# A plan for operand building and Sinkhorn beside unit 0's end, larger token blocks in unit 0, and a reordered lead-in, in a one-core attention and mixture-of-experts kernel

## The chip, the cores and the metric

The kernel runs on one core of a Trainium2 chip. The metric is the device time of one execution in microseconds (us), median of the runs made. The engines are named as the profile names them: PE is TensorE (its weight loads are PEld), DVE is VectorE, ACT is ScalarE, POOL is GpSimd, and SP is the engine whose queue issues the transfers. Each engine works off its own list of instructions in order; semaphores tie the lists together.

## The reference

Three parts follow each other, all in float32. The attention has 2 batches, 8 heads, 768 tokens and head size 64, so 1536 tokens of width 512 come out of it.

```
k_sum = k.reshape(B, H, nb, 32, D).max(axis=3);  v_sum = v.reshape(B, H, nb, 32, D).mean(axis=3)
scores = concat([where(|i - j| < 16, q k^T / 8, -1e9), q k_sum^T / 8 + log(32)])
x = softmax(scores) @ concat([v, v_sum])                  # (1536, 512)
logits = x @ w_gate;  P = exp(logits - logits.max())      # (1536, 8)
for _ in range(8):                                        # Sinkhorn
    P /= P.sum(1) + 1e-9;  P /= P.sum(0) + 1e-9;  P *= N / E
y = sum over e of P[:, e] * (relu(x @ w1[e]) @ w2[e])      # 8 experts, 512 -> 1024 -> 512
h = y @ w_in                                              # 512 -> 2048
out = ((a0 + a1 h + a2 h^2 + a3 h^3) / (1 + |b0| |h| + |b1| h^2 + 1e-6)) @ w_out
```

## The kernel before

**Numbers in two halves.** Each large float32 operand is held as a high half (`h`) and a low half (`l`, the rest), and each product takes three matmuls (lines 166 to 168 and 948 to 950). `xh` and `xl` are the attention's output, `w1h`, `w1l`, `w2h`, `w2l` the weights, `hh`, `hl` the hidden layer. Making a low half needs its high half first, as a rule on ACT, and then a subtraction on DVE or POOL.

**Units.** The eight experts are cut into 16 units of 512 hidden columns, and the last part into four. Unit 0 runs beside the attention in blocks of tokens. Its jobs stand in the list `mains`: per block four `g1` (one for each 128 hidden columns; 12 matmuls, then ReLU on ACT and `hl` on DVE) and per 128 tokens one `g2` (12 matmuls of 512 columns, copied to `acc` by ACT). Units 1 to 15 run as 30 steps `v`, each over the two halves `j` of the tokens: `block(v, j)` forms its hidden layer by seven products (named by their sums X, Y and Z) of prepared sums instead of eight, and its second layer (`g2w`, tiles `p_v`) is spread over the next block, six jobs of six matmuls. I write block (0,0), (0,1), (1,0) for them.

**Operands of the seven products.** From `xh` and `xl` `t_queue(0..3)` builds `th` and `tl`, each for 192 tokens of both halves: four additions (`parts`, tiles `b`), four differences (`all_sums`), three casts on ACT with three differences (`outs`). `t1_queue(0..3)` rewrites part of `xh`, `xl` (tiles `c`): two additions, a difference, a cast, a difference. On the weights' side `w_sums` (tile `S`, four operations on POOL) and `w_op` (seven per step `v`, tiles `wA` and `wS`, high and low half) and `w2_op` (two per step, `w2h_v` and `w2l_v`, on POOL).

**What sets the order.** Everything is written out by hand: an instruction stands in its engine's list where the Python code comes to it. In the attention there is one round `s` per 64 query tokens: scores of `s`, values of `s-3`, transposition of `s-2`, normalization of `s-1`, exponentials of `s`, the key window of `s+1` (`kw`, POOL), then jobs from `todo` at that round and `main(s, 0.8)` twice, which takes jobs from `mains` as far as their costs fit the credit. `ready` holds a block of unit 0 back until its tokens are through. After the last round the rest of `mains` is taken one by one, with one entry of the list `beside` after each: weights' sums, logits, and the work of `t_queue(0, 1)` and `t1_queue(0, 1)`. The other two of each go in at `step(v)`, two at a time, in block (0,0) and on.

**Sinkhorn.** Ten jobs (`sk_max_b`, `sk_first`, eight `sk_step`) run at calls of `tick`, one call per `step`, six per block. Each `sk_step` sends one small matmul (`csp`) to PE that needs DVE's column sums (`cs`), and DVE then goes on with its result. In the kernel before all ten may run from the first call on.

**The lead-in.** Three groups of 256 keys and one of 256 queries are loaded (`load_nat`), copied to token order (`by_token`, two DVE copies), transposed on PE, placed (`place` for keys, `place_q` for queries) and reduced to block maxima (`block_keys`, DVE), group after group; then the first round starts.

Of the kernel before, what the change touches and what calls it, by code (L numbers as in the profile page):

```python
# [22 lines left out]
def kernel(  # L23
# [244 lines left out]
    with ExitStack() as actx:  # L268
# [83 lines left out]
        def by_token(nm, b, i):  # L352

            t = nat[nm, b, i]
            n = len(ordered)
            g = NTT - 2 * (4 - n if n < 4 else 1 + n % 2)
            ordered.append(n)
            for par in range(2):
                r, x = acc[g + par].rearrange("p (h d) -> p h d", h=H), t[:, :, par, :]
                if n >= 4:  # L360
                    pcopy(r, x)
                else:
                    nc.vector.tensor_copy(r, x)
            nat[nm, b, i] = acc[g:g + 2]
# [118 lines left out]
        load_nat(k, "k", 0, 1)  # L483
        load_nat(k, "k", 0, 2)
        make_identity(nc, ident)
        for j in range(2):
            for t_ in qz:
                nc.gpsimd.memset(t_[j * D:(j + 1) * D, :, :, 1 - j, :], 0.0)
        nc.vector.memset(ones, 1.0)
        nc.vector.memset(wavg, 0.0)  # L490
        for m in (wavg[:, NB - LT // BLK:NB],):
# [11 lines left out]
            nc.vector.memset(t_, 0.0)  # L503
        for t_ in vx:
            nc.vector.memset(t_, 0.0)
        for i, m in enumerate(masks):
            nc.gpsimd.memset(m, 0.0)
            nc.gpsimd.memset(m[:, :, SO:CO], math.log(BLK))
            if i == 0:
                nc.gpsimd.memset(m[:, :, 0:WIN], NEG)  # L510
            if i == 2:
                nc.gpsimd.memset(m[:, :, QT + WIN:WK], NEG)
            for j in range(2):
                mm = m[j * QT:(j + 1) * QT, 0, 0:WK]
                nc.gpsimd.affine_select(
                    out=mm, in_=mm, compare_op=ALU.is_ge, fill=NEG, base=-1,
                    pattern=[[1, WK]], channel_multiplier=-1,
                )
                nc.gpsimd.affine_select(
                    out=mm, in_=mm, compare_op=ALU.is_ge, fill=NEG, base=2 * WIN - 1,  # L520
                    pattern=[[-1, WK]], channel_multiplier=1,
                )

        new_q(0, 0)
        for i in range(NL):
            by_token("k", 0, i)
            load_nat(v, "v", 0, i)
            load_vx(i)
# [3 lines left out]
            if i == 0:  # L532
                by_token("q", 0, 0)
                for par in range(2):
                    place_q(qT[0, 0], par, transpose8("q", 0, 0, par, True))
                window(0, 1)
            block_keys(0, i)
        load_nat(q, "q", 0, 1)
        for g in range(2):
            dma_w(0, 1, g)  # L540
        window(0, 2)
        todo = {}
        SW = [3, 3, 4, 4, 4, 4, 5, 5]

        def at(s, f, *args):
            todo.setdefault(s, []).append(lambda: f(*args))


        for i in range(NL):
            at((i + 1) // 3, sum_v, 0, i)  # L550
# [47 lines left out]
        for s in range(NQ + AV):  # L598
            if s < NQ:
                scores(s)  # L600
            if s >= AV:
                av(s - AV)
                if s - AV + 3 < NQ:
                    load_vx(s - AV + 3)
            if 0 <= s - AV + 1 < NQ:
                trans(s - AV + 1)
            if 0 < s <= NQ:
                norm(s - 1)
            if s < NQ:
# [8 lines left out]
            main(s, 0.8)  # L618
        assert not todo


# [187 lines left out]
    tjobs = {0: [], 1: []}  # L809

    def t_part(nm, i, tag, k, t, eng=None):
        o = i // 2 * HT + t * NW + i % 2 * TPIECE
# [5 lines left out]
    def t_queue(i):  # L818
# [3 lines left out]

        def parts():
            b[11], b[12] = t_part("b11", i, "s1", 0, 0), t_part("b12", i, "s2", 0, 1)
            b[22], b[21] = t_part("b22", i, "s3", 1, 1, nc.vector), t_part("b21", i, "s1", 1, 0, nc.vector)

        def sums(r, x, y):
            nc.vector.tensor_sub(b[r], b[x], b[y])
# [11 lines left out]
            for a in ((1, 12), (0, 22), (2, 21)):  # L840
                out(*a)

        tjobs[i // 2] += [parts, all_sums, outs]

    def t1_queue(i):
        o = i // 2 * HT + NW + i % 2 * TPIECE
# [8 lines left out]
            nc.scalar.copy(h, b[11])  # L855
            nc.vector.tensor_sub(l, b[11], h.bitcast(F32))

        tjobs[i // 2] += [parts, out]

    wop = {}  # L860
    wS = {}
# [61 lines left out]

    def step(v):
        tick(v > 1)
        for f in tjobs[1][:2]:
            f()
        del tjobs[1][:2]

    def block(v, j):  # L930

# [93 lines left out]
                if extra:  # L1025
                    extra(b, c)

    for i in (0, 1):
        t_queue(i)
    for i in (0, 1):  # L1030
        t1_queue(i)
    for i in (2, 3):
        t_queue(i)
    for i in (2, 3):
        t1_queue(i)
    beside = [lambda: w_sums(0), lambda: logit_step(0), lambda: w_op(0, 0), lambda: logit_step(1), lambda: w_op(0, 1)]
    for f in tjobs.pop(0):
        beside.append(f)
    beside[6:6] = [lambda: logit_step(2)]
    beside[9:9] = [lambda: logit_step(3)]  # L1040
    while mains:
# [60 lines left out]
```

## Time and profile before

| what | value |
|---|---|
| median of 3 runs (lowest, highest) | 1456.67 us (1455.76, 1458.33) |
| the profiled execution | 1455.68 us, span of its trace 1454.0 us |
| granted PE clock, mean over the span | 0.981 of full speed |
| first score product (score tile 0) starts | 20.92 us |
| ninth score product (tile 8) starts: mark A | 64.06 us |
| first `g1` of unit 0 after the last attention product | 146.54 us |
| X of block (0,0) starts: mark B | 187.05 us |
| X of block (1,0) starts: mark C | 256.11 us |
| X of block (2,0) starts | 287.39 us |

Times within the trace count from the span's start. Busy time of PE is a sum of overlapping matmuls, so it is read together with the start of the next matmul. A clock of 1.00 is 2.4 GHz, 0.50 is 1.2 GHz.

### The profile page before, as it was taken

What the parts mean: (1) busy time and instruction counts of PE and PEld (TensorE: products, weight loads), DVE (VectorE), ACT (ScalarE), POOL (GpSimd) and SP (SyncE); (2) the same over time, 40 slices, a digit from 0 to 9 for tenths busy, and PEclk for the clock granted to TensorE, in tenths of its full rate; (3) what the DMA queues carried; (4) which work ended last, traced back from release to release, by engine and by line L of the source; (5) the groups of instructions that cost most, each with busy time, mean ns of one, the idle gap of its engine ahead of it and who ended that gap; (6) DMA issues with size and microseconds to landing.
All of it is one profiled execution on the core that took longest, in us unless ns stands there. A gap on an engine that the chain in (4) does not pass through costs nothing.

```text
span 1454.0 us, 19477 instructions
## 1 busy us (share of the span) xinstructions
PE 1382.1 (95%) x7195; PEld 1217.7 (84%) x7195; DVE 1074.5 (74%) x1858; ACT 505.2 (35%) x1106; POOL 839.6 (58%) x1042
## 2 busy tenths in 40 slices
PE   5899946999999999999999999999999999999998
PEld 3778835888898888888888889888888998888886
DVE  5676368567777777767776777777776579999996
ACT  4666321232122122222221222212212258776764
POOL 5641365357677767666776767766766333555541
PEclk9899967999999999999999999999999999999999
DMA  6731001112111222111222122212211110111002
GB/s 160 180 98 40 1 14 44 37 52 62 62 62 60 69 76 62 59 55 62 76 60 68 62 62 62 66 61 77 62 62 52 48 44 1 47 33 38 30 0 87
DMA packets 90094, 85.55 MB, mean 59 GB/s; under 512 B 22928, under 2 KB 70032, under 8 KB 90000
## 3 DMA queue, kind: packets, MB, share of 16 engines
q1 hardware_dynamic: 90000, 84.32, 19.5%
q8 instruction: 57, 0.93, 0.3%
q14 instruction: 37, 0.30, 0.1%
HBM read 72.76 MB, written 11.53 MB: 58 GB/s over the span
## 4 chain that ended last, share of the span: by engine, by line
PE 61%; DVE 20%; POOL 8%; ACT 6%; DMA 2%; issue 2%; SPq 0%; ACTq 0%; POOLq 0%; DVEq 0%
PE p_v L168 10%; PE p_v L167 9%; PE p_v L166 9%; PE X L948 5%; PE X L949 5%; PE X L950 5%; DVE r L206 4%; PE Y L949 2%; PE Y L950 2%; PE Y L948 2%; DVE ta L209 2%; DVE ab L203 2%; DVE ab L192 2%; PE p L166 2%; PE p L167 2%; PE p L168 2%
## 5 line engine op out<-in xcount | busy, mean ns | idle before, releaser
L1009 DVE SCALAR_TENSOR_TENSOR acc<-p_v,Pt,acc 128x512 f32<-128x512 f32 x336 | 250.1, 744 | 76.8 <-PE p_v L168 75.1
L168 PE MATMUL p_v<-w2h_v,hl_v 128*128 128x512 f32 x720 | 286.4, 398 | 0.0
L167 PE MATMUL p_v<-w2l_v,hh_v 128*128 128x512 f32 x720 | 285.0, 396 | 0.0
L166 PE MATMUL p_v<-w2h_v,hh_v 128*128 128x512 f32 x720 | 282.0, 392 | 0.0
L956 ACT ACTIVATE hh_v<-s 128x384 fp32r<-128x384 f32 x180 | 94.7, 526 | 355.7 <-DVE s L971 202.6
L957 DVE SCALAR_TENSOR_TENSOR hl_v<-s,hh_v 128x384 fp32r<-128x384 f32 x180 | 126.4, 702 | 104.9 <-ACT hh_v L956 104.9
L168 PEld LDWEIGHTS p_v<-w2h_v,hl_v 128*128 128x128 f32 x720 | 135.3, 188 | 28.9
L736 POOL TENSOR_SCALAR ce<-ce 128x256 uint32<-128x256 uint32 x64 | 69.1, 1079 | 152.8 <-DVE ce L730 152.8
L166 PEld LDWEIGHTS p_v<-w2h_v,hh_v 128*128 128x128 f32 x720 | 135.8, 189 | 17.0
L167 PEld LDWEIGHTS p_v<-w2l_v,hh_v 128*128 128x128 f32 x720 | 135.4, 188 | 16.9
L213 POOL TENSOR_TENSOR hl<-ta,hh 128x512 fp32r<-128x512 f32 (+1 forms) x52 | 63.1, 1214 | 141.2 <-ACT hh L212 139.2
L963 ACT COPY s<-X 128x384 f32<-128x384 f32 x60 | 28.8, 480 | 248.5 <-PE X L950 248.5
L111 POOL TENSOR_SCALAR wS<-S 128x256 fp32r<-128x256 f32 x116 | 57.9, 499 | 98.2 <-PE X L950 96.4
L166 PE MATMUL p<-xh,w1h 128*128 128x512 f32 (+3 forms) x304 | 107.2, 353 | 0.0
L168 PE MATMUL p<-xh,w1l 128*128 128x512 f32 (+3 forms) x304 | 106.0, 349 | 0.0
L167 PE MATMUL p<-xl,w1h 128*128 128x512 f32 (+3 forms) x304 | 106.0, 349 | 0.0
L112 POOL TENSOR_TENSOR wS<-S,wS 128x256 fp32r<-128x256 f32 x120 | 96.4, 804 | 16.3 <-ACT wS L109 6.6
L166 PE MATMUL p<-w2h,hh 128*128 128x512 f32 x240 | 95.3, 397 | 2.4 <-DVE acc L238 2.3
L168 PE MATMUL p<-w2h,hl 128*128 128x512 f32 x240 | 94.3, 393 | 0.1
L167 PE MATMUL p<-w2l,hh 128*128 128x512 f32 x240 | 94.3, 393 | 0.0
L948 PE MATMUL X<-th,wS 128*128 128x384 f32 x240 | 80.8, 337 | 4.9 <-ACT s L963 4.9
L112 POOL TENSOR_TENSOR w2l_v<-sb,w2h_v 128x512 fp32r<-128x512 f32 x60 | 81.0, 1350 | 5.0
(189 smaller groups left out, 3436.1 us busy)
## 6 DMA issues: line engine op xcount, KB each, us to landing
sa<-in_moe_w_dram SPq DMA_DIRECT2D x30, 512.0 KB, 3.5
sb<-in_moe_w_dram SPq DMA_DIRECT2D x30, 512.0 KB, 3.8
cv<-in_moe_w_in_dram SPq DMA_DIRECT2D x32, 256.0 KB, 3.7
cv<-in_moe_w_out_dram SPq DMA_DIRECT2D x32, 256.0 KB, 3.3
f_in<-cf SPq DMA_DIRECT2D x32, 128.0 KB, 2.3
f_out<-cf SPq DMA_DIRECT2D x32, 128.0 KB, 1.8
s<-f_in SPq DMA_DIRECT2D x8, 512.0 KB, 3.4
s<-f_out SPq DMA_DIRECT2D x8, 512.0 KB, 3.6
```

The lines of the kernel that those rows point to most:

```text
L112: nc.gpsimd.tensor_sub(lo, src, hi.bitcast(F32))
L166: nc.tensor.matmul(ps, lhsT=sh, rhs=mh, start=(i == 0), stop=False)
L167: nc.tensor.matmul(ps, lhsT=sh, rhs=ml, start=False, stop=False)
L168: nc.tensor.matmul(ps, lhsT=sl, rhs=mh, start=False, stop=(i == n_k - 1))
L213: nc.gpsimd.tensor_sub(hl[:, :n], ta, hh[:, :n].bitcast(F32))
L736: nc.gpsimd.tensor_scalar(out=e, in0=e, scalar1=896, scalar2=0, op0=ALU.subtract, op1=ALU.max)
L948: nc.tensor.matmul(ps, lhsT=w[:, 0, t], rhs=mh, start=start and t == 0, stop=False, **go)
L949: nc.tensor.matmul(ps, lhsT=w[:, 0, t], rhs=ml, start=False, stop=False, **go)
L950: nc.tensor.matmul(ps, lhsT=w[:, 1, t], rhs=mh, start=False, stop=t == 1, **go)
L956: nc.scalar.activation(hh, src, AF.Relu)
L957: nc.vector.scalar_tensor_tensor(out=hl, in0=src, scalar=0.0, in1=hh.bitcast(F32), op0=ALU.max, op1=ALU.subtract)
L1009: nc.vector.scalar_tensor_tensor(out=a, in0=ps, scalar=Pt[:, g, e:e + 1], in1=a, op0=ALU.mult, op1=ALU.add)
```

## The change

Five things are altered.

1. Lead-in: of the two copies of `by_token` one goes to ACT, of the two placings of a key group one goes to DVE; `place_q` moves behind the copy of the second key group; masks 1 and 2 and the zeroing of the second query buffer are made later (the mask of the last rows in round 4); the second query group is loaded into a staging tile and so ahead of the value groups' use; it is transposed in round 2 instead of 3.
2. Unit 0's weights are split in rounds 3 to 6, two parts each, before in rounds 3 to 5 (two, four, two).
3. Unit 0's token blocks are 256, 256, 256, 384, 384, before 128, 128, 256, 256, 384, 384. The credit per round goes from 1.6 to 1.4.
4. After the last round a table `plan` of eleven groups is laid over the remaining jobs of `mains` up to the last `g1`. It holds `t_queue(0..2)`, `parts` and `all_sums` of the fourth, and `t1_queue(0, 1)`. Two of the four additions of `parts` move from DVE to POOL. Five pieces (`rest`) are left for the first five `step`s.
5. Sinkhorn's ten jobs get due calls 4, 6, 8, 10, ... 22.

```diff
         def load_nat(src, nm, b, i):
-            if (nm, b, i) == ("q", 0, 0):
-                t = apool.tile([P, NP, LT], F32, tag="kT", name="q_0_0", bufs=4)
+            if nm == "q" and b == 0 and i < 2:
+                if i:
+                    t = spool.tile([P, KC, 2 * P], F32, tag="stg", name="q_0_1")
+                else:
+                    t = apool.tile([P, NP, LT], F32, tag="kT", name="q_0_0", bufs=4)
...
-                if n >= 4:
+                if n >= 5:
                     pcopy(r, x)
+                elif par:
+                    nc.scalar.copy(r, x)
                 else:
                     nc.vector.tensor_copy(r, x)
...
+        def place_k(i):
             new_k(0, i)
             for par in range(2):
-                place(kT[0, i], par, transpose8("k", 0, i, par, True), 1.0, True)
+                place(kT[0, i], par, transpose8("k", 0, i, par, True), 1.0)
...
-        SW = [3, 3, 4, 4, 4, 4, 5, 5]
+        SW = [3, 3, 4, 4, 5, 5, 6, 6]
...
+        at(4, make_mask, 2)
...
-        order = [(3, "q", 0, 1)] + [(8 + i, "k", 1, i) for i in range(NL)]
+        order = [(2, "q", 0, 1)] + [(8 + i, "k", 1, i) for i in range(NL)]
...
-        for n in (P, P, 2 * P, 2 * P, HB, HB):
+        for n in (2 * P, 2 * P, 2 * P, HB, HB):
...
-            main(s, 0.8)
+            main(s, 0.7)
...
-        if g2q and g2q[0][0] <= point[0] or len(jobs) > 9 or not g2q:
+        if g2q and g2q[0][0] <= point[0] or not g2q:
             run_job()
...
-    jobs += [(0, sk_max_b), (0, sk_first)]
-    jobs += [(0, lambda i=i: sk_step(i == 7)) for i in range(8)]
+    jobs += [(4, sk_max_b), (6, sk_first)]
+    jobs += [(8 + 2 * i, lambda i=i: sk_step(i == 7)) for i in range(8)]
...
-            b[22], b[21] = t_part("b22", i, "s3", 1, 1, nc.vector), t_part("b21", i, "s1", 1, 0, nc.vector)
+            b[22], b[21] = t_part("b22", i, "s3", 1, 1), t_part("b21", i, "s1", 1, 0)
...
     def step(v):
         tick(v > 1)
-        for f in tjobs[1][:2]:
+        for f in rest[:1]:
             f()
-        del tjobs[1][:2]
+        del rest[:1]
...
+    plan = [
+        [lambda: logit_step(0), T[0][0]],
...
+        [T[3][1]],
+    ]
+    g1s = len(mains) - HB // P
...
+    for m in range(len(mains)):
         mains.pop(0)[2]()
-        if beside:
-            beside.pop(0)()
-    for f in beside:
-        f()
-    for i in range(2, len(OPS)):
-        w_op(0, i)
+        while plan and m + 1 >= g1s * (12 - len(plan)) // 11:
+            for f in plan.pop(0):
+                f()
+        if m == g1s - 1:
+            assert not plan
+            for i in range(2, len(OPS)):
+                w_op(0, i)
     dma_sub(1, 1)
+    rest = [T[3][2], T[6][0], T[7][0], T[6][1], T[7][1]]
```

How the table moves instructions shows at two engines. First DVE at unit 0's end. `hl_768_0` is the low half of unit 0's hidden layer for the block that starts at token 768, `b_0` are the tiles of `t_queue(0)`, `tl` its results, `Pt` the logits. Before:

```order
L181 SCALAR_TENSOR_TENSOR hl_768_2_1838<-p_0_768_2_1824,hh_768_2_1837 128x384
L181 SCALAR_TENSOR_TENSOR hl_768_3_1858<-p_0_768_3_1844,hh_768_3_1857 128x384
L649 TENSOR_TENSOR Pt<-Pt,lgt_1861 128x32
L815 TENSOR_TENSOR b_0_1914<-xh,xl 128x384
L815 TENSOR_TENSOR b_0_1916<-xh,xl 128x384
L649 TENSOR_TENSOR Pt<-Pt,lgt_1932 128x32
L181 SCALAR_TENSOR_TENSOR hl_1152_0_1964<-p_0_1152_0_1950,hh_1152_0_1963 128x384
L828 TENSOR_TENSOR b_0_1910<-b_0_1912,b_0_1910 128x384
```

Of the change:

```order
L674 TENSOR_TENSOR Pt<-Pt,lgt_1716 128x32
L853 TENSOR_TENSOR b_0_1689<-b_0_1691,b_0_1689 128x384
L853 TENSOR_TENSOR b_0_1691<-b_0_1693,b_0_1691 128x384
L853 TENSOR_TENSOR b_0_1693<-b_0_1693,b_0_1689 128x384
L853 TENSOR_TENSOR b_0_1695<-b_0_1695,b_0_1693 128x384
L181 SCALAR_TENSOR_TENSOR hl_768_0_1774<-p_0_768_0_1760,hh_768_0_1773 128x384
L181 SCALAR_TENSOR_TENSOR hl_768_1_1791<-p_0_768_1_1777,hh_768_1_1790 128x384
L858 TENSOR_TENSOR tl_1652<-b_0_1691,th_1649 128x2x192
```

The differences of `t_queue(0)` stand eight jobs of unit 0 earlier, ahead of the block at token 768 instead of behind the first `g1` of the block at 1152, and the additions are gone from DVE's list.

Second POOL in block (0,0). `wA_1` and `wS_1` are weight operands of step 1, `b_2`, `b_3`, `c_2`, `c_3` tiles of `t_queue` and `t1_queue`, `w2h_v_0` the first second-layer weight, which the first `g2w` needs. Before:

```order
L815 TENSOR_TENSOR b_2_2150<-xh,xl 128x384
L815 TENSOR_TENSOR b_2_2152<-xh,xl 128x384
L111 TENSOR_SCALAR wA_1_2168<-sa_2126 128x256
L112 TENSOR_TENSOR wA_1_2168<-sa_2126,wA_1_2168 128x256
L815 TENSOR_TENSOR b_3_2188<-xh,xl 128x384
L815 TENSOR_TENSOR b_3_2190<-xh,xl 128x384
L111 TENSOR_SCALAR wS_1_2213<-S_2140 128x256
L112 TENSOR_TENSOR wS_1_2213<-S_2140,wS_1_2213 128x256
L815 TENSOR_TENSOR c_2_2260<-xh,xl 128x384
L815 TENSOR_TENSOR c_2_2262<-xh,xl 128x384
L111 TENSOR_SCALAR w2h_v_0_2273<-sb_1256 128x512
```

Of the change:

```order
L111 TENSOR_SCALAR wA_1_2120<-sa_2088 128x256
L112 TENSOR_TENSOR wA_1_2120<-sa_2088,wA_1_2120 128x256
L840 TENSOR_TENSOR c_2_2124<-xh,xl 128x384
L840 TENSOR_TENSOR c_2_2126<-xh,xl 128x384
L111 TENSOR_SCALAR wS_1_2145<-S_2102 128x256
L112 TENSOR_TENSOR wS_1_2145<-S_2102,wS_1_2145 128x256
L840 TENSOR_TENSOR c_3_2149<-xh,xl 128x384
L840 TENSOR_TENSOR c_3_2151<-xh,xl 128x384
L111 TENSOR_SCALAR w2h_v_0_2177<-sb_1120 128x512
```

Four additions of `t_queue(2)` and `t_queue(3)` no longer stand here; four of `t1_queue` still do, between the weights' operations.

## Rows read from the trace of the kernel before

**Rows 1.** The page's table of 40 slices of 36.35 us: PE's line.

```profile
PE   5899946999999999999999999999999999999998
```

**Rows 2.** Windows between marks: length; PE, PEld, DVE, ACT, POOL busy (count); PEclk; DMA.

```profile
0.00:20.92 20.92, 7.57 (x32) 6.27 (x33) 10.91 (x21) 6.30 (x9) 10.80 (x37) 1.00 0.82 201
20.92:64.06 43.14, 33.59 (x251) 28.61 (x252) 25.86 (x51) 24.58 (x91) 28.93 (x45) 0.88 0.57 141
64.06:146.54 82.48, 77.33 (x764) 67.62 (x762) 58.38 (x130) 52.83 (x192) 23.11 (x49) 0.98 0.36 86
146.54:187.05 40.51, 40.51 (x208) 35.66 (x205) 16.29 (x32) 13.79 (x30) 12.39 (x13) 1.00 0.00 1
187.05:256.11 69.06, 36.54 (x141) 31.25 (x140) 49.92 (x119) 13.25 (x30) 41.48 (x51) 0.70 0.10 31
256.11:287.39 31.28, 31.28 (x158) 28.12 (x157) 15.83 (x26) 6.66 (x14) 11.45 (x17) 1.00 0.09 26
```

**Rows 3.** Waits from B to C: who waited for whom, us, times, longest.

```profile
PE csp L686 <- DVE cs L682: 27.7, 6, 9.3
...
DVE b L828 <- POOL b L815: 9.8, 1, 9.8
...
POOL S L872 <- DMA sa<-in_moe_w_dram: 3.0, 1, 3.0
```

**Rows 4.** Timeline of the lead-in: start, us, engine, line, operation.

```profile
11.77 1.01 DVE L363 COPY acc<-k 128x512 f32<-128x512 f32 x2
...
20.59 0.27 POOL L289 TENSOR_SCALAR kw<-ks 128x96 f32<-128x96 f32 x1 [8.09 <-DVE ks L342]
...
22.85 0.37 SPq L298 DMA_DIRECT2D q<-in_q_dram  x1
...
38.84 2.03 PE L428 MATMUL sc<-kw,qz 128*128 128x120 f32 x8 [4.30 <-DVE qz L328]
```

**Rows 5.** Timeline from 47 to 60 us: SP and POOL.

```profile
48.77 0.46 SPq L298 DMA_DIRECT2D q<-in_q_dram  x1
...
53.17 2.50 POOL L112 TENSOR_TENSOR w2l<-s,w2h 128x512 fp32r<-128x512 f32 x2 [1.26 <-ACT w2h L109]
...
58.70 0.27 POOL L289 TENSOR_SCALAR kw<-ks 128x96 f32<-128x96 f32 x1
```

**Rows 6.** Timeline of PE: the first matmul of a job and what follows it.

```profile
66.93 0.30 PE L166 MATMUL p<-xh,w1h 128*128 128x128 f32 x1
...
68.30 1.10 PE L428 MATMUL sc<-kw,qz 128*128 128x120 f32 x8
...
89.95 0.36 PE L166 MATMUL p<-xh,w1h 128*128 128x256 f32 x1
...
91.46 1.05 PE L428 MATMUL sc<-kw,qz 128*128 128x120 f32 x8
...
184.33 0.39 PE L166 MATMUL p<-w2h,hh 128*128 128x512 f32 x1
...
187.05 0.33 PE L948 MATMUL X<-xh,wA 128*128 128x384 f32 x1
```

**Rows 7.** Chain of work in late attention rounds: start, us, what.

```profile
127.07 0.57 DVE a L435
...
130.70 0.57 DVE a L435
```

**Rows 8.** Timeline of POOL in block (0,0).

```profile
198.86 0.74 POOL L872 TENSOR_TENSOR S<-sa 128x256 f32<-128x256 f32 x1 [3.00 <-DMA sa<-in_moe_w_dram]
...
209.93 2.58 POOL L815 TENSOR_TENSOR c<-xh,xl 128x384 f32<-128x384 f32 x2
...
213.49 1.45 POOL L112 TENSOR_TENSOR w2l_v<-sb,w2h_v 128x512 fp32r<-128x512 f32 x1
```

**Rows 9.** Timeline of DVE: one pair of additions at two times.

```profile
158.14 1.02 DVE L815 TENSOR_TENSOR b<-xh,xl 128x384 f32<-128x384 f32 x2
...
192.00 1.88 DVE L815 TENSOR_TENSOR b<-xh,xl 128x384 f32<-128x384 f32 x2
```

More of the change, by code (lines that the diff above doesn't have):

```diff
@@ L485, with zero_q, make_mask @@
         make_identity(nc, ident)
-        for j in range(2):
-            for t_ in qz:
+        def zero_q(t_):
+            for j in range(2):
                 nc.gpsimd.memset(t_[j * D:(j + 1) * D, :, :, 1 - j, :], 0.0)
+        def make_mask(i):
+            m = masks[i]
+            nc.gpsimd.memset(m, 0.0)
+            nc.gpsimd.memset(m[:, :, SO:CO], math.log(BLK))
+            if i == 0:
+                nc.gpsimd.memset(m[:, :, 0:WIN], NEG)
+            if i == 2:
+                nc.gpsimd.memset(m[:, :, QT + WIN:WK], NEG)
+            for j in range(2):
+                mm = m[j * QT:(j + 1) * QT, 0, 0:WK]
+                nc.gpsimd.affine_select(
+                    out=mm, in_=mm, compare_op=ALU.is_ge, fill=NEG, base=-1,
+                    pattern=[[1, WK]], channel_multiplier=-1,
+                )
+                nc.gpsimd.affine_select(
+                    out=mm, in_=mm, compare_op=ALU.is_ge, fill=NEG, base=2 * WIN - 1,
+                    pattern=[[-1, WK]], channel_multiplier=1,
+                )
+        zero_q(qz[0])
         nc.vector.memset(ones, 1.0)
@@ L505 @@
             nc.vector.memset(t_, 0.0)
[L506 to L528, printed above, removed]
+        make_mask(0)
+        def place_k(i):
             new_k(0, i)
             for par in range(2):
-                place(kT[0, i], par, transpose8("k", 0, i, par, True), 1.0, True)
[L532 to L537, printed above, removed]
@@ L538 @@
-        load_nat(q, "q", 0, 1)
-        for g in range(2):
-            dma_w(0, 1, g)
+                place(kT[0, i], par, transpose8("k", 0, i, par, True), 1.0)
+        new_q(0, 0)
+        by_token("k", 0, 0)
+        load_nat(v, "v", 0, 0)
+        load_vx(0)
+        by_token("q", 0, 0)
+        place_k(0)
+        window(0, 1)
+        block_keys(0, 0)
+        make_mask(1)
+        by_token("k", 0, 1)
+        load_nat(v, "v", 0, 1)
+        for par in range(2):
+            place_q(qT[0, 0], par, transpose8("q", 0, 0, par, True))
@@ L541 @@
+        place_k(1)
+        block_keys(0, 1)
+        by_token("k", 0, 2)
+        load_nat(v, "v", 0, 2)
+        load_nat(q, "q", 0, 1)
+        load_vx(1)
+        load_vx(2)
+        dma_w(0, 1, 0)
+        dma_w(0, 1, 1)
+        place_k(2)
+        block_keys(0, 2)
         window(0, 2)
+        zero_q(qz[1])
         todo = {}
-        SW = [3, 3, 4, 4, 4, 4, 5, 5]
+        SW = [3, 3, 4, 4, 5, 5, 6, 6]
         def at(s, f, *args):
@@ L549 @@
         for i in range(NL):
-            at((i + 1) // 3, sum_v, 0, i)
+            at(i // 2, sum_v, 0, i)
         at(2, prep_v, 0)
@@ L617 @@
                 window(QB)
-            main(s, 0.8)
+            main(s, 0.7)
         assert not todo
@@ L801, in sk_step @@
             sk_row()
-    jobs += [(0, sk_max_b), (0, sk_first)]
-    jobs += [(0, lambda i=i: sk_step(i == 7)) for i in range(8)]
+    jobs += [(4, sk_max_b), (6, sk_first)]
+    jobs += [(8 + 2 * i, lambda i=i: sk_step(i == 7)) for i in range(8)]
     TPIECE = HT // 4
-    tjobs = {0: [], 1: []}
+    tjobs = {}
     def t_part(nm, i, tag, k, t, eng=None):
@@ L841, in outs @@
                 out(*a)
-        tjobs[i // 2] += [parts, all_sums, outs]
+        tjobs[i] = [parts, all_sums, outs]
     def t1_queue(i):
@@ L856, in out @@
             nc.vector.tensor_sub(l, b[11], h.bitcast(F32))
-        tjobs[i // 2] += [parts, out]
+        tjobs[4 + i] = [parts, out]
     wop = {}
@@ L1026, in unit @@
                     extra(b, c)
-    for i in (0, 1):
+    for i in range(4):
         t_queue(i)
-    for i in (0, 1):
         t1_queue(i)
[L1032 to L1041, printed above, removed]
-        mains.pop(0)[2]()
-        if beside:
-            beside.pop(0)()
-    for f in beside:
-        f()
-    for i in range(2, len(OPS)):
-        w_op(0, i)
+    T = tjobs
+    plan = [
+        [lambda: logit_step(0), T[0][0]],
+        [lambda: w_sums(0), lambda: logit_step(1)],
+        [T[0][1], T[1][0]],
+        [T[0][2], lambda: logit_step(2), lambda: w_op(0, 0)],
+        [T[1][1], T[2][0], lambda: w_op(0, 1)],
+        [T[1][2], lambda: logit_step(3), T[4][0]],
+        [T[2][1], T[5][0]],
+        [T[2][2], T[3][0]],
+        [T[4][1]],
+        [T[5][1]],
+        [T[3][1]],
+    ]
+    g1s = len(mains) - HB // P
+    assert g1s >= len(plan)
+    for m in range(len(mains)):
+        mains.pop(0)[2]()
+        while plan and m + 1 >= g1s * (12 - len(plan)) // 11:
[5 more added lines that the diff above has]
+                w_op(0, i)
     dma_sub(1, 1)
+    rest = [T[3][2], T[6][0], T[7][0], T[6][1], T[7][1]]
     for v in range(NSUB):
```

## The prediction

> **What bounds the kernel now.** I read the page's slices first, then the windows between the marks, then the waits in the one window that stands out, then single timelines. The slices show PE near full from the eighth of 40 on up to the last one; the holes are in the first slice and in the sixth and seventh [rows 1]. The windows measure them [rows 2]. Up to the first score product PE is busy for 7.57 of 20.92 us. From there to mark A it is busy for 33.59 of 43.14 us at a clock of 0.88. From A to the end of the attention it is nearly full, and from there to mark B there is no hole at all (40.51 of 40.51), while DVE is busy for 16.29 us and POOL for 12.39 us. From B to C, blocks (0,0) and (0,1), PE is busy for 36.54 of 69.06 us, and that at a clock of 0.70, while DVE has 49.92 and POOL 41.48 us of work. The next two blocks, with the same matmuls and six `g2w` jobs more, take 31.28 us. So the hole to be closed lies between B and C. The waits name it [rows 3]: PE waits 27.7 us for Sinkhorn's column sums, because DVE has operands, Sinkhorn and hidden layers in one list; DVE in turn waits 9.8 us for POOL's additions, and POOL 3.0 us for the weights of step 1. In the stretch ahead of B the same two engines are idle more than half of the time.
>
> **The change, part by part.** I add up three stretches: start to A, A to B, B to C.
>
> *Start to A: 64.06 to 58.* In the lead-in the rounds of keys follow each other on DVE: the second copy stands at 11.77 us behind the first reduction, and the window that closes the lead-in at 20.59 us [rows 4]. Per round the copy pair (1.01 us) is halved by ACT, half of the placing goes to DVE, and the query placing no longer stands between two reductions. I take 1 us for each of two rounds and 0.3 us more: first score product at 18.6. The second query group was asked for at 22.85 us, and the fifth score product waited for its placing until 38.84 us [rows 4]; loaded and transposed one round earlier it can start at about 32. From there POOL's list decides: eight low halves at 1.25 us (a pair takes 2.50 [rows 5]), the third mask, the copies of the next queries and four windows. By my count the key window of tile 8, now done at 58.70 + 0.27 us [rows 5], is done at 55. In between SP holds it up: the third query group is asked for behind the last weights of unit 0, which wait for a free staging tile, now at 48.77 us [rows 5] and then at about 44, so it lands near 48. PE then has a transposition, tile 7's products and the first 256-column `g1` to do, partly at the lower clock, and A comes at 58. Bounds: 55 if PE adds nothing, 62 if only the lead-in's gain is kept. A wait that grows here has behind it on POOL all later windows, and behind them PE.
>
> *A to B: 122.99 to 127.* A `g1` of 128 columns takes 68.30 - 66.93 = 1.37 us, one of 256 columns 91.46 - 89.95 = 1.51 us, a `g2` 187.05 - 184.33 = 2.72 us [rows 6]. Twice the tokens for 10% more: the larger blocks save 8 x 1.37 - 4 x 1.51 = 4.9 us in all. But they start later, so by A fewer of them are done. After A there were 4 small and 8 larger `g1` and 5 `g2` to do in the attention and its tail; now there are 11 larger `g1` and 6 `g2`: 3 x 1.51 + 2.72 - 4 x 1.37 = 1.8 us more. Late rounds take 130.70 - 127.07 = 3.63 us [rows 7] when they hold a `g1`, and that is a loop over DVE's scores, ACT's exponentials, ReLU and `hl`, not PE. With the credit cut some rounds hold no job and others a `g2`, so PE's idle time there, now 82.48 - 77.33 = 5.15 us [rows 2], may grow; I take 2 us. Sum: 126.8. The last part of this stretch, from the first job after the attention on, is 40.51 + 1.51 + 2 x 2.72 = 47.5 us of PE work. Beside it now stand 20 POOL additions (1.29 us each at worst, 2.58 a pair [rows 8]), `w_sums` (four at 0.74) and seven low halves, together 34 us; on DVE 16 differences and 13 operations of the outputs, 29 at between 0.51 and 0.94 us [rows 9], about 20 us beside the hidden layer's eight `hl`. Both fit, and each group waits for one that stands a `g1` or two ahead, while three result tiles let PE run ahead by two jobs. So I cost the build at nothing here. If that cover fails, every microsecond that DVE's list is late with an `hl` beyond two jobs is one of PE.
>
> *B to C: 69.06 to 33.* Without any wait it is 31.28 less six `g2w` of six matmuls: 31.28 - 6 x 2.72 / 2 = 23.1 us. What is left in block (0,0) weighs on POOL. Its list after B: `w_sums` (3 us; it needs the weights of step 1, which are asked for when the last weight operands are split, and I take them to land at B, since now POOL stands 3.0 us for them [rows 3]), four additions (5.2 us), three weight operands (two operations each of the size of one of `w_sums`, 1.3 us together, so 3.9 us) and the two second-layer weights (0.62 + 1.45 us each [rows 8] for the second part), 16 us together. PE would come to the first `g2w` after nine. It waits for the second of these weights: 7 us. I add 1.5 us for matmuls at the lower clock behind this gap, as the 0.70 of the window shows it now [rows 2], and 1.4 us for Sinkhorn and the X tile. Sum 33.0. Sinkhorn's stall itself goes: between two `sk_step`s there now lie two calls, a third of a block or some 5 us, for a dozen short operations on DVE. What is late next is `w2_op`. Bounds: 25 when nothing is late, 44 when PE waits for POOL and for Sinkhorn in turn.
>
> *After C.* Sinkhorn's last five steps now lie in blocks (1,0) and (1,1), where PE had no gap. DVE was busy for 15.83 of 31.28 us there [rows 2], so 10 us fit; I take 1 us, and 0 to 4 as bounds.
>
> C then comes at 58 + 126.8 + 33 = 217.8, which is 38.3 us earlier, and with the microsecond after it 37.3. From the profiled 1455.68 that gives 1418.4. The median of the runs lies 1.0 us above the profiled execution: 1419.
>
> **A rule against it.** Two of the four additions of each `parts` move from DVE to POOL. A pair of these additions took DVE 1.02 us when POOL was still, and 1.88 us when POOL was at work [rows 9]. So both engines slow each other, and this work becomes slower beside POOL's. "SBUF — State Buffer" of the Trainium skill (SBUF: two separate sides) puts it harder: a VectorE operation with two SBUF inputs and a GpSimd operation that reads SBUF exclude each other for the whole instruction. The trace's 1.88 us agrees with it.
>
> **The rivals.**
>
> *Full exclusion.* If the two engines can only take turns, their work adds up. Ahead of B: 34 us of POOL and 28 two-input operations of DVE at 0.51 us make 48 of 47.5 us, which just fits. In block (0,0) nine such operations (4.6 us) come on top of POOL's 16. The gap at the first `g2w` grows by about 5 us: 1424. For it: rows 9. Against it: POOL's 1.29 us is already a figure under DVE's load. Chance 0.15.
>
> *The build isn't hidden at unit 0's end.* POOL's additions wait for tiles that DVE's outputs free, DVE's outputs for ACT's casts, and those stand behind ReLUs that wait for PE. If four or five of the eleven groups hold an `hl` back by 3 us beyond the spare, 12 to 15 us are lost: 1431 to 1434. For it: DVE waited 9.8 us for POOL in the same way [rows 3]. Against it: a group stands in front of 2 to 5 us of PE work. Chance 0.15.
>
> *The pile in block (0,0) is not there.* If POOL is done with its groups early and the weights of step 1 land before B, the first `g2w` waits 1 us and not 7, and the clock stays up: C 8 us earlier, 1411, and less if A is at 55. Chance 0.2.
>
> *Slower.* The build may take PE's place ahead of B altogether: `hl` stands in DVE's list behind differences that wait for POOL, PE stops for its result tiles, and the jobs and the build go one after the other. Its price is POOL's 34 plus DVE's 20 us, less what PE still does meanwhile, 6: 48 us at B, 10 more than the gain, 1466. It decides from 38 us of lost PE time on, 3.5 us for each of the eleven groups. Against it: those waits would have to come one behind the other in all eleven. Chance 0.02, and 0.02 that losses in several places end within 0.2%.
>
> **How the numbers follow.** My own case has 0.46: 1419, with 1412 to 1425 for its unknown costs (A at 55 or 62, PE's idle time by 3 us either way). Range: 1405, which takes in the early case with A at 55 (1411 less 3, and 3 us for idle time that shrinks), to 1435, the upper end of the hidden-build rival; what is outside has under 0.2. About 0.2% (2.9 us) is what a measurement of this kernel can tell from no change. Faster by more: 0.96; within: 0.02; slower: 0.02.
>
> **What would show it.** The start of score tile 8 (58), of X of block (0,0) (185) and of block (1,0) (218). From the first job after the attention to B no idle PE; waits for `csp` of under 5 us in all where they were 27.7; the first `p_v` released by POOL's `w2l_v`, and a lower clock right behind it. I am wrong if PE's window ahead of B has holes, if the first `p_v` starts within 10 us of B, or if A comes after 62.

## The result and the profile after

The changed kernel took 1424.36 us (median of 4 runs, 1423.49 to 1425.07) where the kernel before took 1457.47 us beside it: ratio 0.9774, 95% interval 0.9757 to 0.9791, so 33 us faster. 1419 us was predicted, with a range of 1405 to 1435 us. The profiled execution took 1425.07 us with a span of 1423.3 us. Two executions of those below, one of e1 (3703.86 us) and one of the kernel before beside e12 (2776.78 us), took far longer than the others of their kernel and are left out of the ratios. PE's line among the 40 slices, now of 35.58 us, and that of its granted clock:

```profile
PE   6789989999999999999999999999999999999998
...
PEclk7799989999999999999999999999999999999999
```

The two holes in the sixth and seventh slice [rows 1] have become one slice of 8. The windows of the changed kernel between the same marks (columns as in [rows 2]):

```profile
0.00:18.50 18.50, 6.91 (x33) 5.54 (x33) 11.24 (x20) 6.46 (x10) 7.07 (x28) 0.85 0.94 229
18.50:59.71 41.21, 30.81 (x203) 24.12 (x203) 25.15 (x47) 23.50 (x84) 29.12 (x48) 0.65 0.57 133
59.71:139.69 79.98, 72.11 (x716) 63.08 (x714) 58.93 (x130) 52.70 (x194) 24.66 (x53) 0.96 0.40 96
139.69:188.58 48.89, 48.89 (x256) 42.99 (x253) 30.15 (x46) 19.20 (x43) 32.13 (x31) 1.00 0.03 10
188.58:223.46 34.88, 29.80 (x131) 25.09 (x129) 24.46 (x50) 9.38 (x20) 28.41 (x35) 0.85 0.15 47
```

A stands at 59.71, B at 188.58 and C at 223.46 us. B is 1.5 us later than before [rows 2], and C is 32.65 us earlier. So the whole gain stands between B and C: 69.06 us have become 34.88. Ahead of B DVE and POOL are now busy for 30.15 and 32.13 us of a stretch in which PE has no hole (48.89 of 48.89). What is left between B and C, by the waits of this window (who waited for whom, us in total, times, longest):

```profile
DVE tl L858 <- ACT th L857: 4.4, 1, 4.4
...
PE X L973 <- DVE hl_v L982: 3.6, 1, 3.6
...
POOL S L897 <- DMA sa<-in_moe_w_dram: 3.1, 1, 3.1
...
PE p_v L167 <- POOL w2l_v L112: 0.7, 1, 0.7
...
PE X L973 <- ACT s L988: 0.6, 1, 0.6
```

The 27.7 us of waiting for `csp` [rows 3] are gone. In their place PE stands 3.55 us ahead of block (0,1), which the timeline explains (ACT, DVE, POOL and PE, in this order):

```profile
190.22 1.34 ACT L857 CAST th<-b 128x384 fp32r<-128x384 f32 x3
...
190.77 2.58 DVE L858 TENSOR_TENSOR tl<-b,th 128x384 fp32r<-128x384 f32 x3 [4.35 <-ACT th L857]
...
197.93 0.55 DVE L879 TENSOR_TENSOR c<-c,c 128x384 f32<-128x384 f32 x1
199.05 1.38 DVE L881 TENSOR_TENSOR xl<-c,xh 128x384 fp32r<-128x384 f32 x1 [0.58 <-ACT xh L880]
200.35 0.55 DVE L982 SCALAR_TENSOR_TENSOR hl_v<-X,hh_v 128x384 fp32r<-128x384 f32 x1
...
195.09 2.30 POOL L840 TENSOR_TENSOR c<-xh,xl 128x384 f32<-128x384 f32 x2
...
197.06 0.34 PE L975 MATMUL Y<-xh,wS 128*128 128x384 f32 x1
200.95 0.69 PE L973 MATMUL X<-xh,wA 128*128 128x384 f32 x1 [3.55 <-DVE hl_v L982]
...
207.07 0.79 PE L167 MATMUL p_v<-w2l_v,hh_v 128*128 128x512 f32 x1 [0.74 <-POOL w2l_v L112]
```

Read it from the end. PE needs the X tile back, at 197.4 (200.95 - 3.55). DVE's last `hl_v` of block (0,0) reads it, and comes only at 200.35, behind the first outputs of `t1_queue(2)` (`c`, `xl`), two other `hl_v` and the outputs of the fourth quarter (`tl`). DVE works through this list from 190.77 on with no pause over 0.65 us. It could have begun 4.35 us sooner, but ACT makes the casts of the fourth quarter (190.22) only behind its copy of the X tile, which stands ahead of them in its list. POOL's `c`, ready at 195.09 + 2.30 = 197.39, wasn't the last here, but by 0.54 us only: DVE's `c` started at 197.93. POOL had stood 3.1 us for a transfer. Behind the 3.55 us the matmuls of 384 columns take 0.52 us instead of 0.34 until 210.8, which is the lower level of the clock, 1.2 GHz; the window's mean is 0.85.

### The profile page after: what moved, and what is told of

Same layout as the page of the kernel before. It is cut to its first block, busy times and chain, and to the rows that moved or that the text cites. A ratio compares the mean times of both kernels' runs of the same rounds, so it can differ in the third digit from the quotient of the medians.

```text
span 1423.3 us, 19388 instructions
## 1 busy us (share of the span) xinstructions
PE 1376.4 (97%) x7147; PEld 1210.3 (85%) x7147; DVE 1075.7 (76%) x1846; ACT 505.6 (36%) x1104; POOL 846.9 (60%) x1048
## 4 chain that ended last, share of the span: by engine, by line
PE 62%; DVE 19%; POOL 9%; ACT 5%; DMA 2%; issue 2%; SPq 0%; POOLq 0%; DVEq 0%; ACTq 0%
PE p_v L168 10%; PE p_v L167 10%; PE p_v L166 10%; PE X L973 5%; PE X L974 5%; PE X L975 5%; DVE r L206 4%; PE Y L974 2%; PE Y L975 2%; PE Y L973 2%; DVE ta L209 2%; DVE ab L203 2%; DVE ab L192 2%; DVE ta L196 2%; POOL w2l_v L112 1%
## 5 line engine op out<-in xcount | busy, mean ns | idle before, releaser
L166 PE MATMUL p<-xh,w1h 128*128 128x512 f32 (+2 forms) x288 | 103.3, 359 | 0.0
L168 PE MATMUL p<-xh,w1l 128*128 128x512 f32 (+2 forms) x288 | 102.3, 355 | 0.0
L167 PE MATMUL p<-xl,w1h 128*128 128x512 f32 (+2 forms) x288 | 102.2, 355 | 0.0
```

What stands on the lines that cost most here:

```text
L166: nc.tensor.matmul(ps, lhsT=sh, rhs=mh, start=(i == 0), stop=False)
L167: nc.tensor.matmul(ps, lhsT=sh, rhs=ml, start=False, stop=False)
L168: nc.tensor.matmul(ps, lhsT=sl, rhs=mh, start=False, stop=(i == n_k - 1))
```

## The experiments

Each kernel was compared with the kernel before on the same chip; e1 to e4 ran together, so did e5 to e8 and e9 to e11, and e12 by itself. Ratios are to the kernel before (its medians there, in this order: 1456.38, 1455.54, 1456.58 and 1458.24 us).

### The parts by themselves

**e1, e11: lead-in, weights, blocks and credit alone** (items 1 to 3 of the change). The changed kernel with the tail of before:

```
-    jobs += [(4, sk_max_b), (6, sk_first)]
+    jobs += [(0, sk_max_b), (0, sk_first)]
...
-    plan = [
...
+    beside = [lambda: w_sums(0), lambda: logit_step(0), lambda: w_op(0, 0), lambda: logit_step(1), lambda: w_op(0, 1)]
...
```

> The changed kernel with its lead-in, its token blocks of 256 and 384 and its credit of 0.7, but with the operand build, the parts on DVE and Sinkhorn's due times (all 0) of the kernel before. Theory of the prediction (the terms add up): A at 58 to 60, A to B about 127 less nothing, B at 185 to 187, and B to C as before, 69 us: 1453 to 1457 us. Rival, from the windows of the changed kernel (B stands there at 188.58, where it stood at 187.05): what the lead-in saves is eaten by half clock and idle time of PE in the attention, so B comes at 188 to 189 and the time is 1457 to 1460 us. Second rival: the longer stretch of PE work ahead of B already gives the build of before more cover, and B to C shrinks by 8 us: 1447 to 1450 us.

1453.69 us, 0.9980 (0.9967 to 0.9994): faster by 0.2%, no more. Its profile comes from e11, the same kernel:

> The first of these runs again for a profile that can be set beside the others: lead-in, blocks and credit of the changed kernel, with the build of before. Its time was 3 us below before. Theory: mark A comes at 58 to 61 and B at 178 to 181, because the stretch ahead of B then holds no additional waits (40 to 42 us of work after the attention), and B to C takes 65 to 70 us as before, so the lead-in's gain is lost there. Rival: B comes at 184 to 188, as in the changed kernel, and B to C keeps its length: the lead-in's gain is lost in the attention.

1452.94 us in that one execution. Its windows from the end of the attention to B and from B to C:

```profile
139.96:188.89 48.93, 48.93 (x253) 42.84 (x254) 19.31 (x38) 16.02 (x34) 13.73 (x14) 1.00 0.00 1
188.89:254.51 65.62, 35.34 (x141) 30.13 (x139) 46.51 (x115) 12.64 (x29) 39.52 (x49) 0.71 0.10 32
```

B comes at 188.89, not at 178 to 181, and later even than the rival's 184 to 188: by B nothing is gained. B to C is 3.4 us shorter than before [rows 2]. What these parts do is to end the attention earlier and to leave 48.9 us of PE work behind it, where 40.51 were [rows 2].

**e2: plan and due times alone** (items 4 and 5). The kernel before with the changed `plan`, `rest`, `parts` and due times.

> The kernel before with only the build laid out by the plan, all four parts on POOL and Sinkhorn's due times; lead-in, token blocks (128, 128, 256, ...) and credit 0.8 as before. Theory of the prediction: this part carries the whole gain, C at 220 to 223, time 1422 to 1426 us, if the 40.5 us of PE work ahead of B cover the build. Rival: the shorter stretch doesn't cover some 34 us of POOL and 20 us of DVE work; PE gets holes of 5 to 10 us ahead of B and the gap in block (0,0) grows: 1430 to 1440 us.

1429.73 us, 0.9820 (0.9805 to 0.9834). The windows of the same two stretches:

```profile
149.30:195.66 46.36, 43.55 (x206) 36.41 (x205) 31.19 (x43) 17.57 (x40) 33.04 (x31) 0.96 0.04 12
195.66:230.43 34.77, 29.79 (x131) 24.72 (x130) 23.82 (x50) 9.29 (x20) 28.37 (x35) 0.85 0.13 45
```

B to C is as short as in the changed kernel. But here the build isn't covered: PE is idle for 2.8 of 46.36 us, in waits for hidden layers (`hh` 1.5 us, `hl` 1.2 us), and loses clock, and the stretch takes 6 us more than the 40.51 us that the same jobs took before [rows 2]. So the time lies between theory and rival. (A came at 67.56 in this execution, with code that is unchanged up to there; see the last section.)

**e3: due times alone.** The kernel before with these:

```
-        if g2q and g2q[0][0] <= point[0] or len(jobs) > 9 or not g2q:
+        if g2q and g2q[0][0] <= point[0] or not g2q:
-    jobs += [(0, sk_max_b), (0, sk_first)]
-    jobs += [(0, lambda i=i: sk_step(i == 7)) for i in range(8)]
+    jobs += [(4, sk_max_b), (6, sk_first)]
+    jobs += [(8 + 2 * i, lambda i=i: sk_step(i == 7)) for i in range(8)]
```

> The kernel before with only Sinkhorn's due times (4, 6, 8, 10, ... 22). PE waited 27.7 us for Sinkhorn's column sums there. Theory: those waits stand for the whole pile on DVE (operand build, Sinkhorn, hidden layers in one list), so with Sinkhorn out of the way about half of them turns into waits for the build: 1438 to 1446 us. Rival: Sinkhorn's round trips alone are the stall, and it goes with them: 1428 to 1433 us. Second rival: no gain, the pile alone sets the time: 1452 to 1458 us.

1445.03 us, 0.9919 (0.9898 to 0.9940), 11 us less, as its theory has it. B to C takes 57.12 us. PE's waits in it show what the `csp` waits had covered:

```profile
PE X L948 <- ACT s L974: 12.9, 1, 12.9
PE X L948 <- ACT s L963: 5.0, 1, 5.0
PE Y L948 <- DVE s L977: 4.6, 1, 4.6
PE X L948 <- DVE hl_v L957: 2.2, 1, 2.2
```

With Sinkhorn out of the way the operands are late: PE waits 24.7 us where it was idle for 69.06 - 36.54 = 32.5 [rows 2], ACT 12.5 us for DVE's sums and DVE 9.7 us for POOL's additions.

**e7: all but the due times.** The edit of e3 undone in the changed kernel.

> The changed kernel with Sinkhorn's due times back at 0 (and the rule that runs a step early while over nine are left), so that its steps follow each other at every call in block (0,0) and (0,1). Theory: with the build out of DVE's list the steps still come closer together than DVE's dozen short operations between two column sums take, so PE waits 1 to 2 us for each of eight: 8 to 16 us more than the changed kernel, 1432 to 1440 us. Rival 1: DVE is free enough and the due times are worth nothing: 1423 to 1427 us. Rival 2: they are the whole of the 27.7 us that PE stood before: 1448 us and more.

1435.36 us, 0.9866 (0.9845 to 0.9886), 13 us more than e5 beside it. From B to C:

```profile
PE csp L711 <- DVE cs L707: 14.0, 6, 3.8
```

**e8: blocks and credit undone.** `(P, P, 2 * P, 2 * P, HB, HB)` and 0.8 again.

> The changed kernel with unit 0 in blocks of 128, 128, 256, 256, 384, 384 tokens and a credit of 0.8 again; lead-in, plan and Sinkhorn's due times stay. Without lead-in and blocks the plan left PE 2.3 us idle ahead of B, in a stretch that took 46.36 us for 40.45 us of work. Theory: the blocks and the credit are there for cover, 6 to 8 us more PE work beside the build, so without them PE has holes ahead of B again: 1427 to 1431 us. Rival 1: the lead-in alone gives the cover (the attention ends earlier): 1423 to 1426 us. Rival 2: the blocks only cost, and the credit holds jobs back for nothing: 1418 to 1421 us.

1426.87 us, 0.9805 (0.9784 to 0.9826), 4.6 us above e5, with intervals that overlap. The stretch ahead of B takes 46.31 us, with PE busy for 43.48, and PE waits there for the same hidden layers as in e2. From e2 this kernel differs by the lead-in and the rounds of the weights, and those intervals overlap too: no run shows what the lead-in is worth.

**e10: the credit alone.** 0.8 for 0.7 in the changed kernel.

> The changed kernel with a credit of 0.8 for each half round in place of 0.7, and nothing else. Theory: the lower credit moves jobs out of the attention to its end, where they cover the build; with 0.8 the stretch of PE work ahead of B shrinks by some 3 to 5 us, the time in the attention shrinks by about as much of PE's idle time and half clock, and it comes out even: 1421 to 1426 us. Rival 1: cover is short and PE gets holes ahead of B: 1427 us and more. Rival 2: the credit of 0.7 only cost idle time in the attention: 1417 to 1420 us.

1422.78 us, 0.9772 (0.9758 to 0.9787): even. The stretch ahead of B:

```profile
140.20:189.13 48.93, 47.15 (x231) 39.91 (x229) 31.13 (x43) 18.67 (x41) 32.73 (x31) 1.00 0.03 9
```

It is as long as the 48.89 us of the changed kernel, though two `g1` of 256 columns (24 matmuls, 3.0 us) have moved into the attention. In their place PE is idle for 1.8 us, in waits for `hl` (1.4 us) and `hh` (0.3 us). The attention from A on takes 79.75 us with them, against 79.98. So the credit does move cover, as the theory has it; but the stretch gets no shorter for it.

### How far the build is covered

**e12: more work for POOL.** Six of POOL's additions ahead of B are done twice, into the same tile.

```
-        (eng or nc.gpsimd).tensor_add(r, a, b)
+        nc.gpsimd.tensor_add(r, a, b)
+        if i < 3 and k == 1:
+            nc.gpsimd.tensor_add(r, a, b)
```

> The changed kernel with six of POOL's additions ahead of mark B done twice (the second two of each of the first three quarters), into the same tile with the same result: 6 to 8 us more work for POOL in the stretch after the attention, where it is busy for 32 of 48.9 us. Theory: the build is hidden there with room to spare, so POOL's idle time shrinks and PE still has no hole ahead of B; at most block (0,0) comes a little later: 1421 to 1426 us. Rival: the build only just fits (the two engines slow each other, and each waits for the other's tiles), so most of the 6 to 8 us comes through to PE: 1427 to 1432 us.

1423.98 us, 0.9773 (0.9753 to 0.9792), no change. The window ahead of B, from the first job after the attention on:

```profile
137.95:188.28 50.33, 49.77 (x256) 42.79 (x253) 32.12 (x46) 19.20 (x43) 38.61 (x37) 1.00 0.03 9
```

POOL took 6.5 us more work than in the changed kernel (32.13), and the same 256 matmuls took 1.4 us more (48.89), half a microsecond of it idle. So POOL had room for most of it. That DVE and ACT have room isn't tested by this; in e10 PE waits for them.

### The rest between B and C

**e5: the changed kernel again**, as the measure for e6 to e8.

> The changed kernel again, beside the next three on the same chip, so that they are compared with it and not across chips. In the first four runs the same code ahead of mark A took up to 3.5 us longer or shorter from one execution to the next, so 1421 to 1427 us is expected.

1422.28 us, 0.9778 (0.9757 to 0.9798).

**e4: everything ahead of B.**

```
+        if m >= g1s:
+            for f in (T[3][2], T[6][0]) if m == g1s else (T[6][1], T[7][0]) if m == g1s + 1 else (T[7][1],):
+                f()
     dma_sub(1, 1)
-    rest = [T[3][2], T[6][0], T[7][0], T[6][1], T[7][1]]
+    rest = []
```

> The changed kernel with the five pieces of the build that it leaves for block (0,0) (the last outputs, the last two parts and their outputs) called beside the three last output jobs of unit 0 instead. Theory: in the changed kernel PE stands 3.55 us for the X tile in block (0,0) because DVE's hidden layer is queued behind these pieces, then 1 us for POOL's second-layer weights, and runs about 10 us at half clock behind that; all of it goes, so 7 to 8 us: 1416 to 1418 us. Rival 1: the wait only moves, to POOL's second-layer weights or to PE ahead of B: 1421 to 1425 us. Rival 2: the waits go but the clock falls anyway: 1419 to 1421 us.

1422.18 us, 0.9773 (0.9755 to 0.9791): no gain, the first rival. The wait moved to an earlier point of block (0,0) (timeline of POOL, DVE, ACT, PE):

```profile
186.35 4.83 POOL L840 TENSOR_TENSOR c<-xh,xl 128x384 f32<-128x384 f32 x4
...
188.99 1.33 DVE L879 TENSOR_TENSOR c<-c,c 128x384 f32<-128x384 f32 x1 [0.90 <-POOL c L840]
...
190.36 0.51 ACT L880 CAST xh<-c 128x384 fp32r<-128x384 f32 x1 [4.55 <-DVE c L879]
...
193.04 0.47 ACT L988 COPY s<-X 128x384 f32<-128x384 f32 x1
...
193.57 0.69 PE L973 MATMUL X<-th,wS 128*128 128x384 f32 x1 [4.82 <-ACT s L988]
```

ACT's copy of the X tile now stands behind a cast that waits for DVE, and that for POOL. One list's late entry holds back what stands behind it on the next.

**e6: additions ahead of B, their outputs later.**

```
+        if m == g1s:
+            T[3][2]()
+            T[6][0]()
+            T[7][0]()
-    rest = [T[3][2], T[6][0], T[7][0], T[6][1], T[7][1]]
+    rest = [lambda: None] * 5 + [T[6][1], T[7][1]]
```

> The changed kernel with the last outputs and the additions of the last two parts called beside unit 0's third-last job, and the outputs of these two parts called later, at the end of block (0,0) and after the first product of block (0,1). With all five pieces ahead of block (0,0) ACT stood 4.55 us for a difference of DVE, and PE 4.82 us for ACT's copy of the X tile behind it. Theory: the additions are ready early, no ACT or DVE instruction of blocks (0,0) stands behind a wait for POOL, and PE neither waits nor falls to half clock: 6 to 8 us below the changed kernel, 1416 to 1418 us. Rival: the wait goes on to POOL's second-layer weights at the first product of the second layer, 3 to 5 us with half clock behind it: 1420 to 1424 us.

1419.62 us, 0.9758 (0.9737 to 0.9778), 2.7 us less than e5, with intervals that overlap. B to C takes 31.48 us; in the six executions that have the changed kernel's code there (the first, e2, e5, e8, e10, e12) it takes 34.28 to 36.00. What is late now is what the prediction had put there:

```profile
PE p_v L167 <- POOL w2l_v L112: 1.6, 2, 0.9
PE p_v L166 <- POOL w2h_v L111: 1.5, 1, 1.5
```

**e9: the second-layer weights first**, on top of e6.

```
-            if v == 0 and i >= 5:
-                w2_op(0, i - 5)
-                if i == 6:
-                    dma_sub(1, 2)
+            if v == 0 and i == 0:
+                w2_op(0, 0)
+                w2_op(0, 1)
+                dma_sub(1, 2)
```

> The kernel of the run before last but two (additions beside unit 0's last jobs, their outputs split over blocks (0,0) and (0,1)) with the two second-layer weights of sub-unit 0 split ahead of the sums and operands of sub-unit 1, at the first product of block (0,0) and not at its last two. There PE still waited 3.1 us for these weights in block (0,1) and ran about 4 us at half clock behind it. Theory: POOL is through with both weights at about 8 us behind mark B, 2 us before PE asks for them, so waits and half clock go: B to C 26 to 28 us instead of 31.48, time 1414 to 1417 us. Rival 1: the wait goes to Sinkhorn's column sums or to a hidden layer on DVE, and the time stays: 1418 to 1421 us. Rival 2: the sums and operands of sub-unit 1 come late for block (1,0) now: 1420 us and more.

1417.94 us, 0.9742 (0.9725 to 0.9760), the lowest median here, but above the 1414 to 1417 of the theory, as B to C is above its 26 to 28 us. Window and waits from B to C:

```profile
187.56:216.67 29.11, 25.35 (x131) 22.16 (x129) 21.42 (x49) 7.85 (x17) 27.90 (x36) 1.00 0.17 58
```

```profile
PE csp L711 <- DVE cs L707: 2.4, 2, 1.3
PE X L973 <- DVE hl_v L982: 0.7, 1, 0.7
PE X L973 <- ACT s L988: 0.6, 1, 0.6
```

The waits for POOL and the lower clock are gone. Of the rivals the first shows in part: 2.4 us went to `csp`. The interval still touches that of e5 and overlaps that of e6; the shorter stretch (29.11 us where the changed kernel's code took 34.28 to 36.00) is what shows the gain.

## Why the prediction was right

The sign, the place and the size held. C was put at 217.8 and came at 223.46; the 5.7 us are three small errors of the same sign. In the other execution of the same kernel (e5) A stood at 58.95, B at 184.93 and C at 220.93, so part of it is the spread of executions. Luck has a part in the size: the terms between B and C were off by more than their sum, and the median lies 0.7 us below the profiled execution, where I had put it 1.0 us above.

**Start to A, 58: measured 59.71.** First score product 18.50 (18.6 predicted), fifth 34.46 (32). POOL was done with tile 8's key window at 58.37 and not at 55. One step that failed is the third query group: it was to land near 48, but the last weights wait for a staging tile until 46.92, it was issued at 47.33, and POOL waited for it until 52.83. That wait was 1.53 us of the 3.4; what made the rest isn't traced. A is still in the bounds of 55 to 62.

**A to B, 127: measured 128.87.** PE's idle time in the attention rose from 82.48 - 77.33 = 5.15 [rows 2] to 79.98 - 72.11 = 7.87 us, 2.7 where I took 2. The stretch without a hole is 48.89 us (47.5; it holds one `g1` more than I counted). That the build costs nothing there is right for this kernel. POOL has room for more (e12), but the cover as a whole is close: with 3.0 us less of PE's work PE stands 1.8 us (e10). What I had not seen is that this cover has a worth: I booked larger blocks and cut credit as 4 us of loss, and with both undone (e2, e8) the same plan loses some 6 us ahead of B. The credit alone comes out even (e10). The larger blocks also save PE 4.9 us by the prediction's sum, which is a rival to the cover: with the old build it brought little (e1, 0.2% together with the lead-in), but no run separates the two under the plan.

**B to C, 33: measured 34.88, by other terms.** PE's work was 25.4 us (e9, at full clock, nearly without waits), not 23.1: Sinkhorn's matmuls and restarts are in it, which I had as 1.4 on top. The idle time was 34.88 - 29.80 = 5.1 us and not 7, and it stood for the most part at the X tile, ahead of block (0,1), and only for 0.95 us at the second of the second-layer weights (`w2h_v` 0.21, `w2l_v` 0.74). The first `p_v` started 15.1 us behind B, at 203.68, and nothing of POOL's released it, against the sign that I had named. So the step that failed is where PE meets the pile: I let it pass block (0,0) and wait for POOL's `w2_op`, and it had been held by DVE's list, behind ACT's, before POOL's turned up. With its outputs moved later (e6) PE met the second-layer weights as the prediction has it, for 3.1 us. The lower clock cost 29.80 - 25.4 = 4.4 us and not 1.5: I took it for a tail of the wait, and it lasted 10 us. An idle term 1.9 us too large and a clock term 2.9 us too small cancel in part, which is why 33 came so near.

**Sinkhorn.** That its stall goes is right: its due times are worth 11 us alone (e3) and 13 us on top of the plan (e7). Neither gives the whole: all but the due times 20 us (e7), the due times alone 11, all 33.

**After C, +1.** X of block (2,0) starts 255.94 - 223.46 = 32.48 us behind C, 1.2 us more than before [rows 2]. PE has no hole there; it is 168 matmuls instead of 158, the five `sk_step`s' own, which B to C now lacks. It is work moved, not DVE's lateness.

**The rivals.** *Full exclusion* gave 1424, which the time matches. The match isn't shown to come from its mechanism: the gap that was to grow, at the first `g2w`, wasn't there. Two groups beside each other and by themselves (timeline of the changed kernel: DVE's sums and POOL's low halves, then POOL's sums of weights and DVE's outputs with the other engine still):

```profile
182.24 4.17 DVE L853 TENSOR_TENSOR b<-b,b 128x384 f32<-128x384 f32 x4
...
182.93 2.06 POOL L112 TENSOR_TENSOR wS<-S,wS 128x256 fp32r<-128x256 f32 x2
184.95 1.05 POOL L112 TENSOR_TENSOR wA<-sa,wA 128x256 fp32r<-128x256 f32 x1
...
144.72 0.74 POOL L898 TENSOR_TENSOR S<-S,sa 128x256 f32<-128x256 f32 x1
...
157.78 1.49 DVE L858 TENSOR_TENSOR tl<-b,th 128x384 fp32r<-128x384 f32 x3
```

From 182.24 to 186.41 DVE does four operations that take 0.50 us each alone (1.49 / 3), and POOL about four that take 0.74: 5.0 us of work in 4.17. So DVE takes twice and POOL 1.4 times its time, and they still gain a little by running together. The Trainium skill, "SBUF — State Buffer" (SBUF: two separate sides), has a DVE operation with two SBUF inputs and a POOL operation that reads SBUF fully block each other for the whole instruction; the trace agrees as to the pairing and nearly as to the size. The pairing shows at `hl_v` (beside POOL's work, and with POOL still):

```profile
194.47 1.09 DVE L982 SCALAR_TENSOR_TENSOR hl_v<-s,hh_v 128x384 fp32r<-128x384 f32 x1 [0.65 <-ACT hh_v L981]
...
258.17 0.56 DVE L982 SCALAR_TENSOR_TENSOR hl_v<-s,hh_v 128x384 fp32r<-128x384 f32 x1 [1.34 <-ACT hh_v L981]
```

The `hl_v` at 200.35 took 0.55 us, though POOL's `c` of `t1_queue(3)` ran beside it; one of its two inputs, the X tile, is in PSUM. Ahead of B the slowing was hidden: PE had no hole there. Behind B it wasn't all hidden: in the list that PE waited for, `tl` took 2.58 us instead of 1.49, the two other `hl_v` 1.09 and 1.20 instead of 0.56, and `xl` 1.38 where others took 0.70, 2.9 us together. How much of the 3.55 us that made isn't shown, since POOL's `c` was ready only 0.54 us sooner; no run has the plan with two additions per `parts` back on DVE. *Build not hidden*: refuted for this kernel, seen in e2 and e8 at 6 us instead of the 12 to 15 I gave it. *Pile absent*: it was there; taking it away (e9) gives 1418 where I had said 1411, since Sinkhorn's 2.4 us come up and A and B were later than I took them. *Slower* and *no change* were not seen.

## What to carry to other kernels

When several engines' lists meet in a hole of PE, removing the wait that the profile names brings only the part that no other list holds back: here 27.7 us of named waits were worth 11 us alone. Work that is moved beside PE needs PE work of its own length there: with 40.5 us of it the plan lost some 6 us (e2, e8), with 48.9 nothing. Shifting PE work there isn't free either; for the credit alone it came out even (e10). Within a group, call early what the slowest engine (POOL) has to start, and late what the engines that PE waits for (ACT, DVE) do with it; calling all of it early moved the wait and gained nothing (e4). The other order shows in the stretch from B to C (e6, e9) and in the time less clearly.

## What the runs showed of the hardware that was not expected

**The same code, 3 us apart.** From A to the end of the attention the changed kernel took 79.98 us in one execution and 77.20 us in another (e5). Of the first, then of the second the window from 74 to 82 us:

```profile
74.00:82.00 8.00, 6.52 (x44) 6.20 (x44) 5.39 (x8) 2.73 (x7) 1.25 (x4) 0.57 0.00 0
```

```profile
74.00:82.00 8.00, 7.57 (x57) 5.10 (x58) 6.48 (x12) 4.31 (x14) 1.03 (x3) 1.00 0.32 86
```

In both PE waits at a transposition of queries for DVE's `kT`; again the first, then the second:

```profile
75.48 1.09 PE L313 MATMUL qps<-ident,acc 128*128 128x128 f32 x4 [2.73 <-DVE kT L320]
```

```profile
74.43 0.63 PE L313 MATMUL qps<-ident,acc 128*128 128x128 f32 x4 [2.21 <-DVE kT L320]
```

Behind the 2.73 us PE ran at half clock, behind the 2.21 us it didn't. The other executions go the same way: 79.97 us at a mean clock of 0.96 (e11), 76.24 us at 1.00 (e6). Between B and C the clock fell behind single waits of 3.55 (changed kernel) and 2.59 us (e10), and behind 0.71, 1.52 and 0.85 us close together (e6), and stayed up where no wait was over 1.3 us (e9).

**A lower clock whose cost doesn't show.** From the first score product to A the mean clock was 0.65 in the changed kernel, 0.79 in e10 and 0.83 in e5, and the stretch took 41.21, 41.49 and 39.95 us. PE is idle for 10 to 12 us of it in each, and the lengths don't follow the clock. That PE waits there for POOL's windows in any case would explain it, but no run shows it.

**A spread ahead of the change.** In e2 A came at 67.56 us and in e3 at 67.67, 3.5 us later than in the kernel before [rows 2], with the same code up to there. A difference of that size between single executions at a mark early in the program says nothing by itself; medians of several runs were needed for every verdict under 5 us here.
